# Linear attention with decay, then a gelu MLP, on one core: a new order of GpSimd's work while group 0's MLP runs

## The chip, the cores and the metric

One core of a Trainium2 chip runs the whole kernel. The metric is the time of one execution in device microseconds (us); of several runs the median is given. TensorE is called PE, VectorE DVE, ScalarE ACT, GpSimd POOL and SyncE SP, as in the profile.

## What is computed

An attention without softmax, with a decay per head, over 4 sequences of 768 positions and 8 heads of 64; then an MLP of 512 to 2048 to 512 with exact gelu on the 3072 rows that come out.

```python
for b in range(nb):                       # blocks along the sequence
    intra = (q_b @ k_b.T) * Dmask         # lam ** (i - j) for i >= j, else 0
    out_b = intra @ v_b + (q_b * lam ** (pos + 1)) @ kv_state
    kv_state = lam ** block * kv_state + (k_b * lam ** (block - 1 - pos)).T @ v_b
h = x @ w_in                              # x: [3072, 512], out of all heads
y = gelu(h) @ w_out
```

## The kernel before, in words

The sequence is cut into 24 chunks of 128 positions: chunks 0 to 5 are the first sequence, 6 to 11 the second, and so on (sb is the chunk's place in its sequence, 0 to 5). Four chunks (M = 4) make a group, 512 rows of the MLP, so there are six groups; while group g goes through the MLP, the attention of the four chunks of group g + 1 is put between the MLP's matmuls. The attention of chunks 0 to 3 runs ahead of everything (the loop at L299).

Each engine runs its instructions in the order in which the program writes them, and waits for another engine only where data or a buffer demands it.

One chunk needs:

- its loads (`load`, L63): three DMAs that POOL issues (k, q, v, float32 in memory, bfloat16 on chip), into pools of 8 buffers each (`qkv`, L48). `prefetch(upto)` (L289) issues the loads of all chunks up to that number that have not been issued.
- kT and qT, chunk transposed. Chunks 0 to 7 do this on PE (`transposes`, L157, into PSUM, copied out by DVE). From chunk 8 on it is done by the DMA crossbar (`dma_transposes`, L170): SP issues kT from k, POOL multiplies q by the decay into q_hat (L175), and SP then issues qT from q_hat. SP also issues the MLP's output DMAs (L253), in the same order of program.
- k_dec, the decayed k (`decay_k`, L146, L155 on POOL), for every chunk but a sequence's last (5, 11, 17, 23).
- `scores` (L178): matmuls kT by qT (L183), masked by DVE (L195); then matmuls k_dec by v (L190, kv_ps) that make the next state, with DVE (L199, L201); then POOL makes `old` (L204), the decayed state for the next chunk.
- `outputs` (L207): state by qT (L213), masked scores by v (L217), and a copy into x_t (L223 DVE).

The MLP of a group (`mlp_blocks`, L226) is 16 blocks of four matmuls x_t by w_in (L235, with gelu on ACT) and 16 blocks of four matmuls g_t by w_out (L247). In group 0 the second half goes through outputs 0 and 1 in turn, then 2 and 3.

The order comes from a list of due times (L318 to L326). Unit is one group's MLP work; the MLP of group g runs from g to g + 1, in steps of 1/32 per block. Each chunk from 4 on has four steps with places `fs` in its quarter:

```python
first, end = (0.66, 1.0) if g == 0 else (0.0, 0.97)
at = lambda f: (g + first + (end - first) * (i + f) / M) * total
fs = (-0.5, 0.0, 0.5, 1.05) if g == 0 else (-1.0, 0.0, 0.35, 0.75)
```

Step kind 0 begins the chunk, issues the crossbar transposes (chunk 8 on), decays k on POOL and calls `prefetch`; kind 1 is the transposes on PE (chunks 4 to 7), kind 2 `scores`, kind 3 `outputs`. Before a block, all steps due by then are written out (L350).

For the chunks around the change the list gives these due times: 4 kind 0 at 0.6175, 4 kind 1 at 0.66, 5 kind 0 and 4 kind 2 at 0.7025, 5 kind 1 at 0.745, 4 kind 3 at 0.749, **8 kind 0 at 0.7575**, 5 kind 2 at 0.7875, 6 kind 0 at 0.7875, 6 kind 1 at 0.83, 5 kind 3 at 0.834, 7 kind 0 and 6 kind 2 at 0.8725, 7 kind 1 at 0.915, 6 kind 3 at 0.919, 7 kind 2 at 0.9575, 9 kind 0 at 1.0, 7 kind 3 at 1.004 (written at the end of group 0, ahead of 9 kind 0), 8 kind 2 at 1.085, 8 kind 3 at 1.182. Chunks 4 to 7 are loaded before (L344).

Of the kernel before, what the change touches and what calls it, by code (L numbers as in the profile page):

```python
# [15 lines left out]
def kernel(  # L16
# [23 lines left out]
    M = 4  # L40
# [22 lines left out]
    def load(n, name):  # L63
        raw[n, name] = qkv_pool.tile([128, H, D], BF16, tag=name, name=f"{name}_t")
        nc.gpsimd.dma_start(raw[n, name], chunk_of(name, n))  # L65
# [73 lines left out]
    def begin(n, early=False):  # L139
        c = Chunk()  # L140
        c.n, c.sb, c.early = n, n % NB, early
        c.sc_tag = "mo" if early and n % 2 else "sc"
        c.q, c.k, c.v = (raw.pop((n, name)) for name in "qkv")
        return c

    def decay_k(c, eng):  # L146

        if c.sb == NB - 1:
            return
        c.k_dec = work_pool.tile([128, H, D], BF16, tag="kd", name="k_dec")  # L150
        if eng is nc.scalar:
            for h in range(H):
                nc.scalar.activation(c.k_dec[:, h, :], c.k[:, h, :], ACT.Copy, scale=lam_k[:, h:h + 1])
        else:
            eng.tensor_mul(c.k_dec, c.k, lam_k[:, :, None].to_broadcast((128, H, D)))  # L155

    def transposes(c):  # L157
        t_ps = bank([128, 2, HP, C], BF16, "mh" if c.early else "t", "t_ps")
        for i, src in ((0, c.k), (1, c.q)):
            for hp in range(HP):  # L160
                nc.tensor.transpose(t_ps[:, i, hp, :], src[:, 2 * hp:2 * hp + 2, :], ident)  # L161
        c.kT = work_pool.tile([128, HP, C], BF16, tag="kT", name="kT")
        c.qT = work_pool.tile([128, HP, C], BF16, tag="qT", name="qT")
        if c.early:
            nc.scalar.copy(c.kT, t_ps[:, 0])
        else:
            nc.vector.tensor_copy(c.kT, t_ps[:, 0])  # L167
        nc.vector.tensor_mul(c.qT, t_ps[:, 1], lam_q)  # L168

    def dma_transposes(c):  # L170
        c.kT = work_pool.tile([128, HP, C], BF16, tag="kT", name="kT")
        c.qT = work_pool.tile([128, HP, C], BF16, tag="qT", name="qT")
        q_hat = work_pool.tile([128, H, D], BF16, tag="qh", name="q_hat")
        nc.sync.dma_start_transpose(out=c.kT, in_=c.k.rearrange("p h d -> p (h d)"))
        nc.gpsimd.tensor_mul(q_hat, c.q, lam_p[:, :, None].to_broadcast((128, H, D)))  # L175
        nc.sync.dma_start_transpose(out=c.qT, in_=q_hat.rearrange("p h d -> p (h d)"))

    def scores(c):  # L178
        sc_ps = [bank([128, HP, C], F32, c.sc_tag, f"sc_ps{hi}") for hi in range(2)]
        for hp in range(HP):  # L180
            for hi in range(2):
                p = slice(hi * D, (hi + 1) * D)
                nc.tensor.matmul(sc_ps[hi][:, hp, :], c.kT[p, hp, :], c.qT[p, hp, :], start=True, stop=True)  # L183
        more = c.sb < NB - 1
        if more:
            kv_ps = bank([128, HP, D], F32, "t", "kv_ps")
            for hp in range(HP):
                for hi in range(2):
                    h = 2 * hp + hi
                    nc.tensor.matmul(kv_ps[hi * D:(hi + 1) * D, hp, :], c.k_dec[:, h, :], c.v[:, h, :],  # L190
                                     start=True, stop=True)
        c.sc_m = work_pool.tile([128, HP, 2, C], BF16, tag="sc_m", name="sc_m")
        dmask_r = dmask.rearrange("p (hp hi) i -> p hp hi i", hi=2)
        for hi in range(2):
            nc.vector.tensor_mul(c.sc_m[:, :, hi, :], sc_ps[hi], dmask_r[:, :, hi, :])  # L195
        if more:
            new = work_pool.tile([128, HP, D], BF16, tag="state", name="state")
            if c.sb == 0:
                nc.vector.tensor_copy(new, kv_ps)  # L199
            else:  # L200
                nc.vector.tensor_add(new, kv_ps, states[c.n][1])  # L201
            old = work_pool.tile([128, HP, D], F32, tag="old", name="old")
            if c.sb < NB - 2:
                (nc.vector if c.early else nc.gpsimd).tensor_mul(old, new, lam_c_b)  # L204
            states[c.n + 1] = new, old

    def outputs(c, x_t, off):  # L207
        o_ps = bank([128, HP, C], F32, "o", "o_ps")
        if c.sb > 0:
            for hp in range(HP):  # L210
                for hi in range(2):
                    p = slice(hi * D, (hi + 1) * D)
                    nc.tensor.matmul(o_ps[p, hp, :], states[c.n][0][p, hp, :], c.qT[p, hp, :],  # L213
                                     start=(hp == 0), stop=False, skip_group_check=True)
        for hp in range(HP):
            for hi in range(2):
                nc.tensor.matmul(o_ps[hi * D:(hi + 1) * D, hp, :], c.v[:, 2 * hp + hi, :], c.sc_m[:, hp, hi, :],  # L217
                                 start=(c.sb == 0 and hp == 0), stop=True, skip_group_check=True)
        x_o = x_t[:, :, off * C:(off + 1) * C]
        if c.early:  # L220
            nc.scalar.copy(x_o, o_ps)  # L221
        else:
            nc.vector.tensor_copy(x_o, o_ps)  # L223
# [65 lines left out]
    def prefetch(upto):  # L289
        while next_load[0] <= min(upto, NCH - 1):  # L290
            for name in "kqv":
                load(next_load[0], name)
            next_load[0] += 1
# [26 lines left out]
    for n in range(M, NCH):  # L320
        g, i = n // M - 1, n % M
        first, end = (0.66, 1.0) if g == 0 else (0.0, 0.97)
        at = lambda f: (g + first + (end - first) * (i + f) / M) * total
        fs = (-0.5, 0.0, 0.5, 1.05) if g == 0 else (-1.0, 0.0, 0.35, 0.75)
        todo += [(at(f), kind, n) for kind, f in enumerate(fs)]
    todo.sort()  # L326

    def step(kind, n):
        g = n // M - 1
        if kind == 0:  # L330
            live[n] = begin(n)
            if g > 0:
                dma_transposes(live[n])
            decay_k(live[n], nc.gpsimd)
            prefetch(n + 5)
        elif kind == 1:
            if g == 0:
                transposes(live[n])
        elif kind == 2:
            scores(live[n])  # L340
        else:
            outputs(live[n], xT[g + 1], n % M)
# [3 lines left out]
    for g in range(NG):  # L346
        if g + 1 < NG:
            alloc_x(g + 1)
        for run, cost in mlp_blocks(g):
            while todo and todo[0][0] <= done:  # L350
                step(*todo.pop(0)[1:])
            run()
            done += cost
        for item in [t for t in todo if t[2] // M == g + 1]:
            todo.remove(item)
            step(*item[1:])
# [30 lines left out]
```

## Time and profile before

| | us |
|---|---|
| median of 3 runs | 239.39 (237.59 to 240.59) |
| the profiled execution, its time | 239.67 |
| its span, first to last instruction | 237.5 |
| PE busy / POOL busy in the span | 209.7 / 111.6 |

The profiled execution is one execution of the same program. Its span is shorter than its time by what lies before the first and behind the last instruction, 2.2 us. All times below are counted from the span's start.

### The profile page before, as it was taken

The numbers are of one execution on the slowest core, as the hardware profiler recorded it, in microseconds if no ns is written. First come the engines' busy times: TensorE is split into PE (matmuls) and PEld (weight loads), VectorE is DVE, ScalarE is ACT, GpSimd is POOL, SyncE is SP. The second block draws the span as 40 slices with busy tenths as digits, with TensorE's granted clock in tenths as the row PEclk, the third lists the DMA queues.
The fourth block names the chain that finished last, engine by engine and source line by source line (L and its number), as shares of the span: only waits on it lengthen the run. The fifth ranks groups of instructions, "written<-read, shape, count | busy, mean of one in ns | idle before, by whom it ended". The sixth has DMA issues, their size and how long they took to land.

```text
span 237.5 us, 3783 instructions
## 1 busy us (share of the span) xinstructions
PE 209.7 (88%) x1528; PEld 102.5 (43%) x1552; DVE 62.7 (26%) x111; ACT 86.0 (36%) x158; POOL 111.6 (47%) x132
## 2 busy tenths in 40 slices
PE   1576999993198999999999999999999999999994
PEld 0355344441044444444444444444444444444453
DVE  3396000264034333132223213222321323100000
ACT  6862365000004552106650125621056510266211
POOL 8997236899717949901684696004403200000000
PEclk9999999999569999999999999999999999999998
DMA  7999999999985999994969999601433101110012
GB/s 51 146 149 199 202 207 159 153 188 138 149 35 135 114 88 95 134 171 110 92 56 101 109 168 170 63 0 47 134 89 68 22 26 65 44 44 0 32 59 88
DMA packets 100272, 24.36 MB, mean 103 GB/s; under 512 B 92960, under 2 KB 97312, under 8 KB 100256
## 3 DMA queue, kind: packets, MB, share of 16 engines
q0 software_dynamic: 79104, 13.64, 79.7%
q1 hardware_dynamic: 21152, 10.50, 20.2%
q8 instruction: 12, 0.20, 0.4%
q14 instruction: 4, 0.03, 0.1%
HBM read 27.27 MB, written 6.29 MB: 141 GB/s over the span
## 4 chain that ended last, share of the span: by engine, by line
PE 70%; POOL 14%; DMA 11%; issue 3%; DVE 0%; ACT 0%; POOLq 0%
PE o_ps L247 30%; PE h_ps L235 30%; DMA w_out_t<-in_moe_w_out_dram 8%; DMA k_t<-in_k_dram 3%; POOL v_t L65 3%; POOL q_t L65 3%; POOL k_t L65 3%; PE o_ps L217 3%; PE sc_ps L183 2%; PE o_ps L213 2%; POOL k_dec L155 2%; PE kv_ps L190 2%; PE o_ps L262 1%; POOL w_in_t L87 1%; POOL w_out_t L91 1%
## 5 line engine op out<-in xcount | busy, mean ns | idle before, releaser
L235 PE MATMUL h_ps<-x_t,w_in_t 128*128 128x512 bf16 x372 | 88.0, 386 | 2.3 <-DVE x_t L223 0.8
L247 PE MATMUL o_ps<-w_out_t,g_t 128*128 128x512 bf16 x356 | 83.7, 385 | 1.8 <-issue 1.7
L237 ACT ACTIVATE g_t<-h_ps 128x512 bf16<-128x512 f32 x96 | 57.3, 597 | 41.0 <-PE h_ps L235 41.0
L235 PEld LDWEIGHTS <-w_in_t 128*128 128x128 bf16 x384 | 36.8, 99 | 45.5 <-issue 4.6
L247 PEld LDWEIGHTS <-g_t 128*128 128x128 bf16 x368 | 34.4, 99 | 40.4 <-issue 1.7
L252 ACT COPY o_sb<-o_ps 128x512 f32<-128x512 f32 x23 | 13.5, 585 | 96.0 <-PE o_ps L247 87.8
L195 DVE TENSOR_TENSOR sc_m<-sc_ps,dmask 128x512 bf16<-128x512 f32 x48 | 30.9, 685 | 62.5 <-PE sc_ps L183 62.5
L204 POOL TENSOR_TENSOR old<-state,lam_c 128x256 f32<-128x256 bf16 x12 | 7.3, 611 | 61.4 <-DVE state L201 35.3
L65 POOL DMA_DIRECT2D q_t<-in_q_dram x24 | 21.4, 894 | 5.4 <-DMA w_out_t<-in_moe_w_out_dram 3.3
L65 POOL DMA_DIRECT2D k_t<-in_k_dram x24 | 22.0, 915 | 3.7 <-DMA w_out_t<-in_moe_w_out_dram 1.7
L65 POOL DMA_DIRECT2D v_t<-in_v_dram x24 | 21.3, 889 | 5.0 <-DMA w_in_t<-in_moe_w_in_dram 1.7
L223 DVE CAST x_t<-o_ps 128x512 bf16<-128x512 f32 x20 | 13.8, 690 | 35.6 <-PE o_ps L217 35.6
L155 POOL TENSOR_TENSOR k_dec<-k_t,lam_k 128x512 bf16<-128x512 bf16 x18 | 19.0, 1058 | 0.0
L175 POOL TENSOR_TENSOR q_hat<-q_t,lam_p 128x512 bf16<-128x512 bf16 x16 | 16.7, 1046 | 0.0
L190 PE MATMUL kv_ps<-v_t,k_dec 128*64 128x64 bf16 x160 | 6.9, 212 | 10.5 <-POOL k_dec L155 9.1
L217 PE MATMUL o_ps<-sc_m,v_t 128*64 128x128 bf16 x192 | 10.8, 240 | 0.0
L183 PE MATMUL sc_ps<-qT,kT 64*128 64x128 bf16 x192 | 10.4, 233 | 0.3 <-DVE qT L168 0.2
L190 PEld LDWEIGHTS <-k_dec 128*64 128x64 bf16 x160 | 4.8, 119 | 12.9 <-POOL k_dec L155 9.3
L161 PE MATMUL t_ps<-ident,k_t 128*128 128x128 bf16 x32 | 4.2, 275 | 6.8 <-DMA k_t<-in_k_dram 6.3
L183 PEld LDWEIGHTS <-kT 64*128 64x128 bf16 x192 | 6.0, 99 | 9.5 <-issue 8.0
L213 PE MATMUL o_ps<-qT,state 64*64 64x128 bf16 x160 | 8.9, 235 | 0.7 <-ACT x_t L221 0.7
L167 DVE COPY kT<-t_ps 128x512 bf16<-128x512 bf16 x4 | 1.7, 424 | 28.2 <-PE t_ps L161 28.1
(39 smaller groups left out, 70.6 us busy)
## 6 DMA issues: line engine op xcount, KB each, us to landing
out_dram<-o_sb SPq DMA_DIRECT2D x23, 256.0 KB, 2.2
k_t<-in_k_dram POOLq DMA_DIRECT2D x24, 128.0 KB, 4.4
q_t<-in_q_dram POOLq DMA_DIRECT2D x24, 128.0 KB, 5.5
v_t<-in_v_dram POOLq DMA_DIRECT2D x24, 128.0 KB, 6.1
w_in_t<-in_moe_w_in_dram POOLq DMA_DIRECT2D x4, 512.0 KB, 8.4
w_out_t<-in_moe_w_out_dram POOLq DMA_DIRECT2D x4, 512.0 KB, 15.4
kT<-k_t SPq DMA_TRANSPOSE x16, 4.0
qT<-q_hat SPq DMA_TRANSPOSE x16, 4.1
```

The lines of the kernel that those rows point to most:

```text
L65: nc.gpsimd.dma_start(raw[n, name], chunk_of(name, n))
L155: eng.tensor_mul(c.k_dec, c.k, lam_k[:, :, None].to_broadcast((128, H, D)))
L175: nc.gpsimd.tensor_mul(q_hat, c.q, lam_p[:, :, None].to_broadcast((128, H, D)))
L183: nc.tensor.matmul(sc_ps[hi][:, hp, :], c.kT[p, hp, :], c.qT[p, hp, :], start=True, stop=True)
L190: nc.tensor.matmul(kv_ps[hi * D:(hi + 1) * D, hp, :], c.k_dec[:, h, :], c.v[:, h, :], start=True, stop=True)
L195: nc.vector.tensor_mul(c.sc_m[:, :, hi, :], sc_ps[hi], dmask_r[:, :, hi, :])
L213: nc.tensor.matmul(o_ps[p, hp, :], states[c.n][0][p, hp, :], c.qT[p, hp, :], start=(hp == 0), stop=False, skip_group_check=True)
L217: nc.tensor.matmul(o_ps[hi * D:(hi + 1) * D, hp, :], c.v[:, 2 * hp + hi, :], c.sc_m[:, hp, hi, :], start=(c.sb == 0 and hp == 0), stop=Tru ...
L223: nc.vector.tensor_copy(x_o, o_ps)
L235: nc.tensor.matmul(h_ps, w_in_t[:, ki, kf * 128:(kf + 1) * 128], x_t[:, ki, :], start=(ki == 0), stop=(ki == NK1 - 1))
L237: nc.scalar.activation(g_t[:, kf, :], h_ps, ACT.Gelu)
L247: nc.tensor.matmul(om[io], g_t[:, kf, io * C:(io + 1) * C], w_out_t[:, kf, :], start=(kf == 0), stop=(kf == NK2 - 1))
```

## The change

In group 0's list, kind 0 of chunk 8 (and of it alone) gets the place -0.45 in its quarter instead of -1.0: its due time goes from 0.7575 to 0.8909. It is then written behind kind 0 of chunks 6 and 7 and behind kind 2 of chunk 6, ahead of kind 1 of chunk 7. `prefetch` is called with n + 4 instead of n + 5, for all chunks.

```diff
@@ -321,7 +321,7 @@
         first, end = (0.66, 1.0) if g == 0 else (0.0, 0.97)
         at = lambda f: (g + first + (end - first) * (i + f) / M) * total
-        fs = (-0.5, 0.0, 0.5, 1.05) if g == 0 else (-1.0, 0.0, 0.35, 0.75)
+        fs = (-0.5, 0.0, 0.5, 1.05) if g == 0 else (-0.45 if n == 2 * M else -1.0, 0.0, 0.35, 0.75)
         todo += [(at(f), kind, n) for kind, f in enumerate(fs)]
@@ -332,7 +332,7 @@
             if g > 0:
                 dma_transposes(live[n])
             decay_k(live[n], nc.gpsimd)
-            prefetch(n + 5)
+            prefetch(n + 4)
```

POOL's order from the decay of chunk 4 to that of chunk 9, written out by these two lists (L*n* the three loads of chunk n, D the decay of k, H the q_hat, O the `old`):

```
before: D4 L8 L9 | L10 | H8 D8 L11 L12 L13 | D6 | D7 | O6 | O7 | H9 D9 L14 | O8
after:  D4 L8 | L9 | D6 L10 | D7 L11 | O6 | H8 D8 L12 | O7 | H9 D9 L13 | O8
```

## Rows read from the trace of the kernel before

**Rows 1.** The page's 40 slices of the span (5.94 us each).
```profile
PE   1576999993198999999999999999999999999994
...
PEclk9999999999569999999999999999999999999998
```

**Rows 2.** Waits of PE: total us, times, longest us.
```profile
PE kv_ps L190 <- POOL k_dec L155: 9.1, 1, 9.1
...
PE kv_ps L190 <- DVE state L201: 1.4, 2, 0.9
```

**Rows 3.** Timeline of PE: start us, us until the last ends, instructions.
```profile
55.07 0.40 PE L183 MATMUL sc_ps<-qT,kT 64*128 64x128 bf16 x8
64.57 0.43 PE L190 MATMUL kv_ps<-v_t,k_dec 128*64 128x64 bf16 x8 [9.11 <-POOL k_dec L155]
...
70.53 0.40 PE L183 MATMUL sc_ps<-qT,kT 64*128 64x128 bf16 x8
...
73.61 2.75 PE L235 MATMUL h_ps<-x_t,w_in_t 128*128 128x512 bf16 x12 [0.79 <-DVE x_t L223]
76.30 0.40 PE L183 MATMUL sc_ps<-qT,kT 64*128 64x128 bf16 x8
...
84.67 0.40 PE L183 MATMUL sc_ps<-qT,kT 64*128 64x128 bf16 x8
```

**Rows 4.** Timeline of POOL, 42 to 74 us.
```profile
49.37 0.88 POOL L65 DMA_DIRECT2D k_t<-in_k_dram  x1
...
52.00 1.08 POOL L175 TENSOR_TENSOR q_hat<-q_t,lam_p 128x512 bf16<-128x512 bf16 x1
53.00 1.07 POOL L155 TENSOR_TENSOR k_dec<-k_t,lam_k 128x512 bf16<-128x512 bf16 x1
53.99 0.92 POOL L65 DMA_DIRECT2D k_t<-in_k_dram  x1
...
62.58 0.87 POOL L65 DMA_DIRECT2D v_t<-in_v_dram  x1 [0.95 <-DMA k_t<-in_k_dram]
63.46 2.05 POOL L155 TENSOR_TENSOR k_dec<-k_t,lam_k 128x512 bf16<-128x512 bf16 x2
...
72.66 0.61 POOL L204 TENSOR_TENSOR old<-state,lam_c 128x256 f32<-128x256 bf16 x1 [6.50 <-DVE state L201]
```

**Rows 5.** Busy time by stretch; columns in the first line.
```profile
core 0: us, PE busy (x) PEld busy (x) DVE busy (x) ACT busy (x) POOL busy (x), PEclk, DMA share, GB/s
40.00:52.00 12.00, 11.12 (x95) 5.69 (x94) 4.26 (x8) 1.58 (x3) 11.30 (x14) 1.00 2.21 164
...
64.57:70.53 5.96, 5.96 (x37) 2.83 (x38) 1.64 (x4) 0.00 (x0) 1.55 (x2) 0.62 1.29 54
...
73.61:106.90 33.29, 32.87 (x245) 15.42 (x249) 8.92 (x15) 11.31 (x19) 23.11 (x26) 1.00 1.41 123
```

**Rows 6.** The chain that ended last, 65 to 71 us: start us, us, what.
```profile
65.00 3.53 PE o_ps L247 x8
68.53 0.76 PE t_ps L161 x8
...
69.63 0.97 PE o_ps L247 x4
```

**Rows 7.** L65 alone: the load of chunk 7's k (us from issue to landing).
```profile
L65 POOL DMA_DIRECT2D k_t<-in_k_dram x1: 876/876/876, 39.8 to 39.8; - x1
...
DMA to landing us min/median/max: 8.2/8.2/8.2
```

**Rows 8.** L65, all 72 loads.
```profile
DMA to landing us min/median/max: 3.3/5.5/18.3
```

**Rows 9.** L174 alone: chunk 8's crossbar transpose of k.
```profile
L174 SPq DMA_TRANSPOSE kT<-k_t x1: 1358/1358/1358, 50.0 to 50.0; - x1
...
DMA to landing us min/median/max: 7.9/7.9/7.9
```

**Rows 10.** Tile qT, all 16 crossbar transposes (the longest is chunk 8's).
```profile
L176 SPq DMA_TRANSPOSE qT<-q_hat x16: 1189/1208/2400, 53.1 to 187.8; - x16
...
DMA to landing us min/median/max: 2.4/4.1/7.3
```

## The prediction

> **What bounds the kernel now.** I read the 40 slices first, to see where PE, the busiest engine, is not full: behind the start there is one hole only, in the tenth and eleventh slice (3 and 1 tenths, 53 to 65 us); the granted clock falls to 5 and 6 tenths in the eleventh and twelfth [rows 1]. Then PE's waits, to see what made the hole: the matmuls of kv_ps waited for k_dec of L155 once, 9.1 us; the next entry for the same matmuls is 1.4 us in the prologue [rows 2]. PE's timeline puts it: the scores of chunk 6 end at 55.47, its kv_ps starts at 64.57 [rows 3]. POOL's timeline says why: k_dec of chunks 6 and 7 run at 63.46, behind q_hat 8 and k_dec 8 (52.00, 53.00) and nine loads from 53.99 on, chunks 11 to 13. Of these the last waited for the landing of an earlier load before POOL could issue it at 62.58 [rows 4]. So POOL spent 11.5 us (52.00 to 63.46) on work for chunk 8 and later, while PE stood. From 73.61 on PE is full, 32.87 of 33.29 us in the first stretch, at clock 1.00 [rows 5]: what is taken out of the hole comes out of the end, as long as PE is not made to wait elsewhere.
>
> **What goes.** (a) k_dec 6. The loads of chunks 8 and 9 end at 49.37 as before, since nothing ahead of them moves. The decay of 6 is next: 49.37 to 50.4, by 1.07 of the k_dec row [rows 4]. Chunk 6's k needs to have landed: PE had transposed it before 55.07, the start of its scores [rows 3]; and chunk 7's k, issued behind it in the same queue, was issued at 39.8 and landed 8.2 later, 48.0 [rows 7]. PE wants k_dec 6 at 55.47. It is there 5 us earlier, and the wait of 9.11 us goes whole [rows 3].
>
> (b) k_dec 7. Load 10 takes what it took, 49.37 to 52.00 = 2.63 [rows 4]: 50.4 to 53.0. The decay of 7 then ends at 54.1, well ahead of its kv_ps (70.53 + 0.33 before, some 11 earlier now, about 59.5).
>
> (c) The clock. In 64.57 to 70.53, 5.96 us in which PE is busy all the time, the clock granted is 0.62 on average, that is mostly 1.2 GHz [rows 5]; ahead of it PE had done nothing for 9.1 us. In 40 to 52, where PE is busy 11.12 of 12.00 us, it is 1.00 (2.4 GHz) [rows 5]. Without the hole I price this stretch at full clock: its 12 matmuls of 128x512 took 3.53 + 0.97 = 4.50 [rows 6], and 12 of the same shape at full clock take 2.75 [rows 3], 1.75 less. The eight transposes took 0.76 [rows 6]; half that at twice the clock gives 0.4 less. The small rest at either clock: 0 to 0.2. I take 2.2 us, with 0 (the clock stays low) and 2.4 as the ends.
>
> Sum of what goes: 9.1 + 2.2 = 11.3 us.
>
> **What is added or moved, and what is late next.** No instruction is added: the same loads, decays and transposes run in another order. What can be late is chunk 8, whose whole kind 0 is moved behind 6 and 7, on POOL, and so also on SP.
>
> When it is needed: group 1 started at 73.61, now 11.3 earlier, 62.3; the scores of 8 at 76.30, now 65.0 [rows 3].
>
> POOL: load 11 follows k_dec 7, 54.1 to 56.7. Next is `old` of chunk 6, which waits for DVE. For chunk 7, where POOL was idle and waiting, `old` started 72.66 - 70.53 = 2.1 behind the start of the scores [rows 3, 4]; for chunk 6 that is 55.07 + 2.1 = 57.2, to 57.8. This is a wait put in front of q_hat 8, of 0.5 us; behind it queue q_hat 8, k_dec 8, load 12, `old` 7, and PE doesn't need any of them before 65. q_hat 8 then runs to 58.9 and k_dec 8 to 59.9: 5 us early.
>
> SP: kT 8 stands between the same two output DMAs of the program as before, and needs only k 8 and a buffer that a chunk before it has left; it is issued at about 50.0 as before and landed 7.9 us later [rows 9]. qT 8 is issued at 58.9 instead of 53.1. The outputs 2 and 3 of group 0 queue behind it on SP, but their last blocks come behind the scores of 7 (70.53 before, about 59.2 now) [rows 3], later than 58.9, so they lose nothing.
>
> Landing of qT 8: its row of before is the longest of 16, 7.3 us; the median is 4.1 and the shortest 2.4 [rows 10]. The 7.3 had kT 8 ahead of it in SP's queue, which landed at 57.9 [rows 9], so qT 8 landed 2.5 behind that. Now kT 8 is down a microsecond before qT 8 is issued. I take the median, 4.1: 63.0, two us before its scores. The ends are 61.3 and 66.2, so a gain of nothing at one end and a wait of 1.2 us at the other.
>
> The Trainium skill ("Advanced Engine Details and Errata", X-Bar Transpose (TRN2)) says that transpose DMAs are as fast as regular ones, at 350-400 GB/s. By its figure a 128 KB transpose would take some 0.4 us of transfer (an estimate of mine), qT 8 could not be late, and rival 1 would fall away with the sum unchanged. The rows of this case speak otherwise, 4.1 us in the middle and 7.9 at most, so the sum stays with the rows.
>
> Loads four instead of five ahead: load n + 4 is issued at kind 0 of chunk n, and wanted at kind 0 of chunk n + 4, one group later, 33.3 us [rows 5]; the longest of 72 landings is 18.3 [rows 8]. Cost nothing; the cover that is left is 15 us. The decays and loads of later groups keep their order otherwise.
>
> Buffers: with load 12 due at chunk 8 instead of 13, POOL no longer asks for a buffer whose chunk is still in work; each load from 12 on takes that of a chunk whose outputs are already written out. Three buffers of k_dec serve 6, 7 and 8, and their owners before (2, 3, 4) are at least two chunks back in PE's order. I put nothing down for it; the other end is one kv_ps of a chunk, 0.4 us [rows 3].
>
> Sum: 237.5 - 11.3 = 226.2 us of span; with 2.2 around it 228.4. The median of before is 0.3 below its profiled execution, so 228.1 for the median.
>
> **The rivals.**
>
> 1. Chunk 8 becomes the new wait. For it: qT 8 is issued 5.8 us later, beside loads 10 to 12. The DMA share, 2.21 in 40 to 52, is the highest of the stretches shown [rows 5], and 7.3 and 7.9 are what chunk 8's transposes took in this very stretch [rows 9, 10]. With 7.9, qT 8 lands at 66.8 and the scores wait 1.8: 228.1 + 1.8 = 229.9. The Trainium skill ("DMA: Bandwidth & Descriptors", Issuing engines are not separate DMA queues) stands on this side: DMAs from SP and POOL run on the same 16 engines and interleave. Against it: kT 8 is no longer ahead in the queue.
>
> 2. The clock stays low although the hole is gone, since the end of group 0 has many small matmuls and short waits: then only (a) is won, 228.1 + 2.2 = 230.3. Against it: 40 to 52 has the same mixture at 1.00 [rows 5].
>
> 3. The change doesn't bring the decay forward: it is held by something that POOL's order doesn't show, a buffer or its k. Then PE waits on, 239.4. Against it: k landed by 48, and POOL ran the decay of 8 without idling before it, in the same pools [rows 4].
>
> 4. Slower. The mechanism is one: qT 8, moved behind the loads, lands as late as the latest load that this trace has, 18.3 us [rows 8], at 58.9 + 18.3 = 77.2. The scores of 8 would wait 12.2 us, and PE's clock would drop behind that wait as it did here, another 2.2: 228.1 + 12.2 + 2.2 = 242.5. It decides the sign from a landing at 65.0 + 11.3 - 2.2 = 74.1 on. Against it: the 18.3 is of a load issued into a queue full of weights, at 20 us, and no transpose took more than 7.9.
>
> **How the numbers follow.** The forecast, 228.1, with a spread of some 1.5 us either way as the three runs of before show it, has 0.85. Rival 1 has 0.06, rival 2 0.04, rival 3 0.03, rival 4 0.02. The range is 225.8 to 230.8: it takes in the forecast's spread, rival 1 and rival 2, and leaves out 3 and 4 and the tails. A measurement of this kernel can tell about 2% (4.8 us) from no change. Faster by more than that: the forecast, rivals 1 and 2, 0.95. Within 2%: rival 3, 0.03. Slower: rival 4, 0.02.
>
> **What the profile after would show.** Right: PE's entry of kv_ps waiting for k_dec of L155 is gone; two k_dec at about 49.4 and 53.0, each followed by three loads; the tenth to twelfth slices full with the clock at 9; group 1's first matmul of L235 at about 62.3 and the scores of chunk 8 at about 65.0 without a wait; q_hat 8 behind `old` 6 at about 57.8. Wrong, if the scores of 8 (L183) wait for a transpose or kv_ps for k_dec 8; if a k_dec row has idle time before it; if the clock in the last 6 us of group 0 is under 1; if any kT of a later chunk waits for a load.

## The result and the profile after

| | before | after |
|---|---|---|
| median, us | 239.99 (4 runs, 237.59 to 241.51) | 227.87 (4 runs, 227.51 to 228.37) |
| ratio, 95% interval | | 0.953 (0.945 to 0.961) |
| the profiled execution, its time | 239.67 | 228.12 |
| its span | 237.5 | 226.1 |

The change makes the kernel 12.1 us faster by the medians, 11.4 us by the two profiled spans. 228.1 was predicted, within 225.8 to 230.8. The ratios here and below leave out an execution that took over 1.5% more than the fastest of its kernel, while the medians are of all: below these are one of "the move only" (232.71), one of "chunk 8 earlier" (234.02) and two of "decays on ACT" (233.19, 233.32).

The 40 slices of after, from its page (5.65 us each):

```profile
PE   1486899989899999999999999999999999999993
...
PEclk9999999999999999999999999999999999999999
```

The hole of two slices and the two slices of low clock behind it [rows 1] are gone. PE's waits after (total us, times, longest us):

```profile
PE t_ps L161 <- DMA k_t<-in_k_dram: 7.2, 3, 5.0
...
PE kv_ps L190 <- DVE state L201: 1.4, 2, 0.9
```

The entry for kv_ps and POOL's k_dec, the longest of before [rows 2], is not there any more; what leads the list now are waits for the first loads in the first 13 us, which were there before as well. The timeline of PE after (start us, us until the last ends):

```profile
54.92 0.40 PE L183 MATMUL sc_ps<-qT,kT 64*128 64x128 bf16 x8
55.25 0.32 PE L190 MATMUL kv_ps<-v_t,k_dec 128*64 128x64 bf16 x8
...
59.09 0.40 PE L183 MATMUL sc_ps<-qT,kT 64*128 64x128 bf16 x8
...
62.17 2.75 PE L235 MATMUL h_ps<-x_t,w_in_t 128*128 128x512 bf16 x12 [0.79 <-DVE x_t L223]
64.85 0.40 PE L183 MATMUL sc_ps<-qT,kT 64*128 64x128 bf16 x8
```

These lines answer to [rows 3]. kv_ps of chunk 6 follows its scores at once. From the scores of 6 to those of 7 it took 70.53 - 55.07 = 15.46 before and takes 59.09 - 54.92 = 4.17 now, 11.29 less. From the scores of 7 to group 1's first matmul it is 3.08 in both, and to the scores of 8 another 2.7 in both. So the gain lies in that one stretch, all but 0.15 us of the 11.4. The timeline of POOL after:

```profile
51.03 1.09 POOL L155 TENSOR_TENSOR k_dec<-k_t,lam_k 128x512 bf16<-128x512 bf16 x1
52.02 0.92 POOL L65 DMA_DIRECT2D k_t<-in_k_dram  x1
...
54.71 1.06 POOL L155 TENSOR_TENSOR k_dec<-k_t,lam_k 128x512 bf16<-128x512 bf16 x1
...
58.39 0.63 POOL L204 TENSOR_TENSOR old<-state,lam_c 128x256 f32<-128x256 bf16 x1
58.96 1.05 POOL L175 TENSOR_TENSOR q_hat<-q_t,lam_p 128x512 bf16<-128x512 bf16 x1
59.96 1.04 POOL L155 TENSOR_TENSOR k_dec<-k_t,lam_k 128x512 bf16<-128x512 bf16 x1
```

The order is that of the prediction, D6, three loads, D7, three loads, `old` 6, q_hat 8, k_dec 8, against [rows 4]. It stands 1.2 to 1.7 us later than worked out, since POOL came to chunk 4's decay later in this execution (44.75, where before it was 42.92); PE's kv_ps, at 55.25, was not touched by that, because D6 was still done three us ahead of it. The clock, by stretch (columns as in [rows 5]), first where it was low before, then group 1:

```profile
55.47:59.30 3.83, 3.83 (x42) 2.01 (x36) 2.92 (x6) 0.11 (x1) 3.82 (x6) 1.00 2.61 145
...
62.30:95.60 33.30, 32.88 (x245) 15.40 (x248) 8.92 (x15) 11.31 (x19) 25.39 (x29) 1.00 1.79 145
```

PE is busy all of the first stretch, at clock 1.00. From kv_ps 6 to the scores of 7 it is now 59.09 - 55.25 = 3.84 us, where the same work took 5.96 at 0.62. (The stretch shown lies 0.2 us behind that.) And chunk 8's last transpose, L176 alone, in the profile after:

```profile
L176 SPq DMA_TRANSPOSE qT<-q_hat x1: 1190/1190/1190, 60.0 to 60.0; - x1
...
DMA to landing us min/median/max: 4.6/4.6/4.6
```

Issued at 60.04 by the timeline of SP, it landed at 64.6; the scores of chunk 8 began at 64.85. In this execution the margin was 0.2 us. (kT 8 had waited 1.5 us on SP for its own k, which POOL had loaded late; no later kT waited for a load.) That is the reading that the experiments start from: the gain is there, but is the new order at its edge?

### The profile page after: what moved, and what is told of

It is laid out like the page before. It is cut to its first block, busy times and chain, and to the rows that moved or that the text cites. A ratio compares the mean times of both kernels' runs of the same rounds, so it can differ in the third digit from the quotient of the medians.

```text
span 226.1 us, 3777 instructions
## 1 busy us (share of the span) xinstructions
PE 206.7 (91%) x1528; PEld 101.5 (45%) x1552; DVE 61.9 (27%) x111; ACT 86.0 (38%) x158; POOL 111.4 (49%) x132
## 4 chain that ended last, share of the span: by engine, by line
PE 87%; DVE 3%; ACT 3%; DMA 2%; issue 2%; POOL 2%; POOLq 0%
PE h_ps L235 38%; PE o_ps L247 35%; PE o_ps L217 4%; PE o_ps L213 3%; PE sc_ps L183 3%; DMA q_t<-in_q_dram 2%; PE kv_ps L190 2%; PE o_ps L262 2%; DVE sc_m L195 1%; PE t_ps L161 1%; ACT k_dec L153 1%; POOL k_t L65 1%; ACT L307 1%; ACT x_t L221 1%; ACT kT L165 0%
## 5 line engine op out<-in xcount | busy, mean ns | idle before, releaser
L247 PE MATMUL o_ps<-w_out_t,g_t 128*128 128x512 bf16 x356 | 82.0, 379 | 1.8 <-issue 1.7
L65 POOL DMA_DIRECT2D q_t<-in_q_dram x24 | 21.5, 895 | 5.9 <-DMA w_out_t<-in_moe_w_out_dram 3.3
L65 POOL DMA_DIRECT2D k_t<-in_k_dram x24 | 22.1, 920 | 3.6 <-DMA w_out_t<-in_moe_w_out_dram 1.7
L65 POOL DMA_DIRECT2D v_t<-in_v_dram x24 | 21.3, 889 | 3.9 <-DMA w_out_t<-in_moe_w_out_dram 1.7
L213 PEld LDWEIGHTS <-state 64*64 64x64 bf16 x160 | 5.5, 113 | 7.5 <-issue 7.1
```

Of the source, the lines that this page charges most:

```text
L247: nc.tensor.matmul(om[io], g_t[:, kf, io * C:(io + 1) * C], w_out_t[:, kf, :], start=(kf == 0), stop=(kf == NK2 - 1))
```

## The experiments

Two theories. **POOL's order**: each engine runs its row in order, so what PE waits for can be worked out by adding up POOL's row; which instruction stands ahead of which is all that counts. **Loads in flight**: it was the number of loads ahead (DMA queues full, landings slow) that cost, and the move is an accessory. The medians, each ratio to the kernel before of its own set:

| kernel | us, median of 4 (lowest to highest) | ratio to before, 95% |
|---|---|---|
| after, again (set 2) | 227.72 (227.68 to 228.29) | 0.952 (0.946 to 0.957) |
| the move only (set 1) | 229.54 (228.84 to 232.71) | 0.956 (0.947 to 0.965) |
| four loads ahead only (set 1) | 236.16 (235.30 to 237.39) | 0.984 (0.978 to 0.991) |
| chunk 8 later (set 1) | 228.64 (227.78 to 228.99) | 0.952 (0.946 to 0.958) |
| chunk 8 earlier (set 2) | 233.25 (230.09 to 234.02) | 0.970 (0.960 to 0.979) |
| decays on ACT (set 1) | 231.73 (229.60 to 233.32) | 0.958 (0.949 to 0.966) |
| decays on ACT, `old` 6 on DVE (set 2) | 228.26 (227.74 to 229.01) | 0.953 (0.948 to 0.959) |
| q_hat 8 ahead of L11 (set 2) | 228.35 (227.69 to 229.46) | 0.955 (0.949 to 0.962) |

Beside them the kernel before ran seven times in each of the two sets: 240.33 (238.51 to 241.72) in set 1, and 239.67 (237.46 to 240.61) in set 2. Where single stretches are set against "after" below, the profile after that is shown above is meant.

**The move alone**, against before:

```diff
-        fs = (-0.5, 0.0, 0.5, 1.05) if g == 0 else (-1.0, 0.0, 0.35, 0.75)
+        fs = (-0.5, 0.0, 0.5, 1.05) if g == 0 else (-0.45 if n == 2 * M else -1.0, 0.0, 0.35, 0.75)
```

> Only kind 0 of chunk 8 is moved; loads stay five chunks ahead. Theory of POOL's order: POOL's row is D4 L8 L9 L10 D6 L11 D7 L12 O6 H8 D8 L13. D6 ends at 53.1 to 54.8, still ahead of the 55.3 at which PE wants it, so the 9.1 us go. One load more stands ahead of q_hat 8: qT 8 is issued 2.6 later than after the change and lands at 65.5 to 67.4, so the scores of chunk 8 wait 0.6 to 2.5 us: 228.7 to 230.6 us. Rival, what cost was the number of loads in flight: they are as many as before, so most of the 9.1 us stays, 235 or more.

229.54, as the order says. Its waits of PE, and its row of POOL:

```profile
PE sc_ps L183 <- DMA qT<-q_hat: 0.9, 1, 0.9
```
```profile
52.30 1.12 POOL L155 TENSOR_TENSOR k_dec<-k_t,lam_k 128x512 bf16<-128x512 bf16 x1
...
55.97 1.09 POOL L155 TENSOR_TENSOR k_dec<-k_t,lam_k 128x512 bf16<-128x512 bf16 x1
...
60.23 1.05 POOL L175 TENSOR_TENSOR q_hat<-q_t,lam_p 128x512 bf16<-128x512 bf16 x1
```

D6 ends at 53.4, still ahead of PE, so the 9.1 us are gone with as many loads ahead as before. What is new is the first line: the scores of chunk 8 wait 0.9 us for qT 8, because q_hat 8 now has one load of three DMAs more in front of it. So the rival of the prediction, chunk 8 as the next wait, does come, with one chunk of loads more.

**Four loads ahead alone**, against before:

```diff
-            prefetch(n + 5)
+            prefetch(n + 4)
```

> Only the loads go to four chunks ahead; kind 0 of chunk 8 stays at -1.0. Theory of POOL's order: D4 L8 L9 H8 D8 L10 L11 L12 D6 D7. D6 ends at 60.5 to 62.1, up to 1.5 more where a load waits for a landing, so PE's wait shrinks from 9.1 to 5 to 8 us and the clock still falls behind it: 233 to 238 us, 235.5 in the middle. Rival, the number of loads in flight: all of the gain, 228.

236.16, inside the first theory's range and far from the rival's 228. Its waits of PE, its row of POOL, and a stretch behind the wait:

```profile
PE kv_ps L190 <- POOL k_dec L155: 5.4, 1, 5.4
```
```profile
50.18 1.04 POOL L175 TENSOR_TENSOR q_hat<-q_t,lam_p 128x512 bf16<-128x512 bf16 x1 [1.32 <-DMA q_t<-in_q_dram]
...
60.05 2.11 POOL L155 TENSOR_TENSOR k_dec<-k_t,lam_k 128x512 bf16<-128x512 bf16 x2
```
```profile
61.22:67.50 6.28, 6.28 (x38) 2.98 (x38) 1.86 (x4) 0.00 (x0) 1.55 (x2) 0.58 0.67 35
```

D6 at 60.05 instead of 63.46 [rows 4]: the load that is not there (2.6 us) and its waits for landings (1.5) are gone, a wait of 1.3 for q 8 to land is new, and POOL's row began 0.4 earlier in this execution. PE's wait shrinks from 9.1 to 5.4, the clock falls behind it all the same, and the work from kv_ps 6 to the scores of 7 takes 6.28 us, no less than before (5.96) [rows 5]. This part of the change alone is worth 4 us (its interval, 0.978 to 0.991, stays under 1, with 2% inside it), the move alone 11; together they are worth 12, since the same wait can go only once.

**Chunk 8 later**, against after:

```diff
-        fs = (-0.5, 0.0, 0.5, 1.05) if g == 0 else (-0.45 if n == 2 * M else -1.0, 0.0, 0.35, 0.75)
+        fs = (-0.5, 0.0, 0.5, 1.05) if g == 0 else (-0.15 if n == 2 * M else -1.0, 0.0, 0.35, 0.75)
```

> The change with kind 0 of chunk 8 later still (-0.15): its q_hat goes behind the old of chunk 7, its crossbar transposes behind one more output DMA. Theory that qT 8 is the next thing to be late, with little margin (it landed 0.2 us before the scores in the profile of after): q_hat 8 ends at about 62.7, qT 8 lands at 67 to 68.5, the scores of chunk 8 wait 2.2 to 3.6 us: 230.3 to 231.7. Rival, the place of chunk 8 doesn't matter once the decays are first: 228.

228.64: a miss of my numbers, though the mechanism is there. The waits of PE, `old` 7 in POOL's row, and qT 8 (L176 alone) in this kernel:

```profile
PE sc_ps L183 <- DMA qT<-q_hat: 0.5, 1, 0.5
```
```profile
61.53 0.61 POOL L204 TENSOR_TENSOR old<-state,lam_c 128x256 f32<-128x256 bf16 x1 [3.55 <-DVE state L201]
```
```profile
L176 SPq DMA_TRANSPOSE qT<-q_hat x1: 1190/1190/1190, 63.2 to 63.2; - x1
...
DMA to landing us min/median/max: 2.4/2.4/2.4
```

qT 8 was issued at 63.2, half a us later than I had put, but landed in 2.4 us, not in the 4.3 to 5.8 that I had put. POOL had stood idle waiting to make the `old` of 7, so no load had been issued since chunk 11's (the last at 55.99, down at 60.7), and the transpose started with no load beside it. Issuing it 3.1 us later than after the change cost PE 0.5.

That the emptied queue is the reason is not shown by this profile alone, but the other landings fit it. In the five profiles in which qT 8 follows the decays, it never landed ahead of the loads that had been issued before it. Where these were still coming down 3.4 us or more behind its issue, it took 4.6 us (after) and 3.9 (the move only); where they were down by 2.5 us behind its issue or sooner, it took 2.4 to 2.7 (chunk 8 later, q_hat 8 ahead of L11, after again).

**Chunk 8 one notch earlier**, against after (-0.55 for -0.45, so that D7 stands behind chunk 8's work and six loads):

```diff
-        fs = (-0.5, 0.0, 0.5, 1.05) if g == 0 else (-0.45 if n == 2 * M else -1.0, 0.0, 0.35, 0.75)
+        fs = (-0.5, 0.0, 0.5, 1.05) if g == 0 else (-0.55 if n == 2 * M else -1.0, 0.0, 0.35, 0.75)
```

> The change with kind 0 of chunk 8 one notch earlier (-0.55): D6 stays first, but D7 now stands behind q_hat 8, k_dec 8, L11 and L12. Theory of POOL's order: D7 ends at 60.5 to 63.2, PE wants it at 59.4, a wait of 1.1 to 3.8 us, and up to 2 more if the clock falls behind it: 229.3 to 233. Rival, only the first decay counts: 228.

233.25, just above the range: the wait is inside what was expected, the clock's price is not. Its timelines of POOL and PE, and the stretches behind the wait:

```profile
60.55 1.09 POOL L155 TENSOR_TENSOR k_dec<-k_t,lam_k 128x512 bf16<-128x512 bf16 x1
```
```profile
59.40 0.40 PE L183 MATMUL sc_ps<-qT,kT 64*128 64x128 bf16 x8
61.69 0.32 PE L190 MATMUL kv_ps<-v_t,k_dec 128*64 128x64 bf16 x8 [1.89 <-POOL k_dec L155]
...
65.39 4.60 PE L235 MATMUL h_ps<-x_t,w_in_t 128*128 128x512 bf16 x12 [0.79 <-DVE x_t L223]
69.92 0.40 PE L183 MATMUL sc_ps<-qT,kT 64*128 64x128 bf16 x8
```
```profile
61.69:65.39 3.70, 2.75 (x27) 1.47 (x29) 1.12 (x2) 0.59 (x1) 3.16 (x5) 0.59 2.87 177
65.39:70.00 4.61, 4.61 (x16) 1.56 (x17) 0.00 (x0) 1.19 (x2) 2.59 (x3) 0.59 1.96 192
```

The wait itself is 1.9 us. But from the scores of 7 to those of 8 it is 69.92 - 59.40 = 10.52 us, against 64.85 - 59.09 = 5.76 after: 4.8 more. What is left beside the wait, 2.9 (I had put up to 2), comes with a clock of 0.59 over the next 8 us, group 1's first 12 matmuls among them (4.60 where they take 2.75). So both decays have to be first, and the place of chunk 8 has an edge on this side that is steeper than on the other.

**The decays of 6 and 7 on ACT**, against before, everything else as it was:

```diff
-            decay_k(live[n], nc.gpsimd)
+            decay_k(live[n], nc.scalar if n in (6, 7) else nc.gpsimd)
```

> The kernel before, with the decays of chunks 6 and 7 made on ACT (eight activations each, 2.7 us by the prologue's rows) and nothing else changed: POOL's loads and chunk 8 stay where they were. Theory of POOL's order: no wait for k_dec is left, but old of chunk 6 is still behind L13 on POOL (63.5); DVE's state of chunk 7 waits for it, the copy of x_t 7 stands behind that on DVE, and group 1 starts at about 65 instead of 62.2: 231. Rival, the loads in flight: nothing gained, 239.

231.73, the median of two executions at 230 and two at 233: eight to ten of the twelve us are won with the loads and chunk 8 where they were, so loads in flight are not what cost. What is left is where the order put it. The two decays on ACT, DVE's timeline and PE's, and the stretch behind PE's wait:

```profile
48.83 3.92 ACT L153 ACTIVATE k_dec<-k_t,lam_k 128x64 bf16<-128x64 bf16 x16
```
```profile
64.84 0.42 DVE L201 TENSOR_TENSOR state<-kv_ps,old 128x256 bf16<-128x256 f32 x1 [3.72 <-POOL old L204]
```
```profile
65.92 4.22 PE L235 MATMUL h_ps<-x_t,w_in_t 128*128 128x512 bf16 x12 [4.21 <-DVE x_t L223]
```
```profile
65.92:70.08 4.16, 4.16 (x13) 1.45 (x13) 0.00 (x0) 1.19 (x2) 4.16 (x6) 0.64 1.85 200
```

DVE's state of chunk 7 waited 3.7 us for `old` 6, which POOL reached only behind L13, and the copy of x_t for which PE waits stands behind that on DVE: 4.21 where after has 0.79. Behind it the clock is 0.64, and from group 1's start to the scores of 8 it takes 4.16 us where after takes 2.68. These 3.4 and 1.5 us account for the profiled execution, which took 233.19, 5 more than the profiled one of after; how they divide in the two executions at 230 is not on record. (A chunk's decay took ACT 2.0 us, not 2.7: the prologue's 2.7 is from one chunk's start to the next.)

**`old` of chunk 6 taken from POOL too**, against the kernel just before:

```diff
-                (nc.vector if c.early else nc.gpsimd).tensor_mul(old, new, lam_c_b)
+                (nc.vector if c.early or c.n == 6 else nc.gpsimd).tensor_mul(old, new, lam_c_b)
```

> The decays of 6 and 7 on ACT as before in e5, and old of chunk 6 on DVE too, so that nothing that group 0 needs stands behind the loads on POOL; the loads stay five ahead and chunk 8 early. Theory: the 3.4 us that e5 lost ahead of group 1 are gone and the time is that of the change, 228 (DVE's 0.4 us more at most). Rival, something else of the old order costs as well: 230 or more.

228.26, and PE's wait ahead of group 1 is back at 0.79:

```profile
62.28 2.75 PE L235 MATMUL h_ps<-x_t,w_in_t 128*128 128x512 bf16 x12 [0.79 <-DVE x_t L223]
```

With the old due times, loads five ahead and the transposes of chunk 8 early, this kernel is as fast as the change within what can be measured. What the change does is thus closed: three small POOL instructions that group 0 needs (D6, D7 and `old` 6) no longer stand behind loads that can wait. Going from five chunks of loads ahead to four does one thing more once chunk 8 is moved: it keeps q_hat 8 early enough, by the 0.9 us that "the move only" shows.

**The loads of chunk 11 behind q_hat 8 and k_dec 8**, against after, to give qT 8 more room:

```diff
-            prefetch(n + 4)
+            if n != 7:
+                prefetch(n + 4)
```

> The change, with the loads of chunk 11 put behind q_hat 8 and k_dec 8 (no loads at kind 0 of chunk 7). Theory: qT 8 is issued 1 us earlier and lands earlier, which takes no wait from PE, since it was already down when the scores began: no change, 228. Rival, the little margin of qT 8 costs in some executions: 0.3 to 1 less.

228.35, no change, as forecast: qT 8 was no wait to begin with. It got its room: issued at 57.9 and down 2.5 us later, it was 3.7 us ahead of the scores of 8 (64.05). **And the change again**:

> The kernel after, again, beside the other runs of this call: 228, and a spread of about 1 us, against 4 us of the kernel before.

227.72, with a spread of 0.6 us. In this profile qT 8 (L176 alone) was quicker, 58.9 to 61.6, and the scores of chunk 8 in PE's timeline began at 65.05, so the margin was 3.4 us, not 0.2:

```profile
L176 SPq DMA_TRANSPOSE qT<-q_hat x1: 1190/1190/1190, 58.9 to 58.9; - x1
...
DMA to landing us min/median/max: 2.7/2.7/2.7
```
```profile
65.05 0.40 PE L183 MATMUL sc_ps<-qT,kT 64*128 64x128 bf16 x8
```

None of the variants beats the change.

## Why the prediction was right

11.3 us of gain were forecast; the two profiled spans differ by 11.4, and the terms came out one by one. The medians differ by 12.1 because the kernel before had a median of 239.99 in these runs, and of 239.39 in the runs that the forecast started from; that the forecast time, 228.1, was met to 0.2 us is in part luck.

**(a) The wait for k_dec 6**: 9.1 predicted, gone whole. That it was POOL's row and not the loads in flight is shown by taking the decays off POOL, and by leaving the loads five ahead.

**(b) k_dec 7**: right, and shown to matter: put behind six loads it costs PE 4.8 us with its clock, in a kernel that is 5.5 slower.

**(c) The clock**: 2.2 predicted. Measured 5.96 - 3.84 = 2.1 for the stretch, at clock 1.00 instead of 0.62. It is a term of its own: with only the wait priced, the forecast would have been 230.3.

**What is late next**: the order of candidates was right, qT 8 first. Its size was off both ways. I had a margin of two us from one landing time, 4.1. The profiles in which it follows the decays show landings from 2.4 to 4.6 (five of them), and a POOL that starts its row up to 2 us earlier or later, so the margin is 0.2 to 3.7. That it was not a wait in the profile after is in part luck. Rival 1 did not come in the change itself, but did with one load more ahead of q_hat 8 (0.9 us).

**The wait that was put in front of q_hat 8**, `old` 6 at 57.2, 0.5 us of it: in the repeated profile POOL was there in time and waited 0.7 us; in the first it came later than the state and did not wait at all. From the repeated profile:

```profile
57.25 0.61 POOL L204 TENSOR_TENSOR old<-state,lam_c 128x256 f32<-128x256 bf16 x1 [0.71 <-DVE state L199]
```

**Outputs 2 and 3 on SP**, "they lose nothing": not quite. In the profile after, ACT had finished output 2 by 59.8, but its DMA went out at 61.28, behind qT 8. Nothing on PE waits for that.

**Loads four ahead, and buffers**: no wait of PE for a load or for a buffer behind the start. Right at nothing.

**The rule on transposes.** The Trainium skill ("Advanced Engine Details and Errata", X-Bar Transpose (TRN2)) says that transpose DMAs are as fast as regular ones. I had held the rows against it, and they do not refute it. They count from issue to landing, with whatever is ahead or beside, and regular DMAs took longer there as well: group 0's first two output DMAs, issued at 46.9 and 48.8 before with loads in flight, took 5.3 to 5.5 us to land, where the median of all is 2.2; the transposes took 7.6 (kT 8) and 4.6 (qT 8) in the profile after, and 2.4 at best. What failed is my step from its bandwidth to a landing: no transpose landed in anything like 0.4 us.

**Rivals 2, 3 and 4**: the clock did come back, the decays did come forward, and no transpose took anything like 18 us (7.6 at most in the profile after).

## What to carry to other kernels

An engine that issues loads and also makes small operands for the busiest engine has one row: add up what stands ahead of each operand (here 2.6 us for the three loads of a chunk) and compare with the time at which it is wanted. Put first what is wanted first, and let the prefetch depth be what still fits behind it. When a wait of TensorE is priced, price the slow stretch behind it too.

## What had not been expected

**The clock's price is not in proportion to the wait.** Behind a wait of 9.1 us the slow stretch cost 2.1 us; behind 5.4 it cost 6.28 - 3.84 = 2.4; behind 4.2 it cost 1.5; behind 1.9 it cost 2.9. (Behind the longer three PE was busy all through the slow stretch; behind the 1.9 it was busy 2.75 of the first 3.70 us.) Behind 0.9 and 0.5 the page shows the clock at full in all slices. [Rows 5] has only the stretch behind the long wait, and says nothing of a short one.

**The spread.** The kernel before varied from 237.5 to 241.7 over all its runs, the kernel after from 227.5 to 228.4. POOL came to chunk 4's decay anywhere from 42.6 to 44.8 us in the profiles. Where PE waits for POOL's row this goes into the time (3.7 to 3.9 us of spread in "decays on ACT", "chunk 8 earlier" and "the move only", though only 2.1 in "four loads ahead only"); where D6 is done three us early it does not. That POOL's lateness is the cause of the spread is an inference from these rows; no run varied it alone.

Where POOL got late can be read. In the profile after, the decay of chunk 3 in the prologue had to wait for PE (so a k_dec row with idle time before it does exist, one of the prediction's signs of being wrong, but ahead of all that the change touches):

```profile
14.85 1.04 POOL L155 TENSOR_TENSOR k_dec<-k_t,lam_k 128x512 bf16<-128x512 bf16 x1 [0.96 <-PE o_ps L217]
```

In the profile of before POOL did not wait there. That is 0.8 us of the 1.8 by which chunk 4's decay was later; the rest came in the loads of chunks 4 to 6, most of which wait on POOL for a load of the weights to land.
